# Rearranging the first loads of a SwiGLU kernel: one x load, a load issued behind the sigmoid, and a transposing load held by a dependency

## Chip, cores, metric

One core of a Trainium2 chip. The metric is the device time of one execution in microseconds (us), as a median over several executions. A lower time is better. Where two kernels are compared, "fast" executions are used: those that are not over 1.5% above the fastest of the same kernel.

## The reference

```python
B, S, D, F = 32, 32, 512, 1792        # x: (32, 32, 512), all bf16
def reference(x, w1, w3, w2):
    gate = jnp.einsum("bsd,df->bsf", x, w1)
    up = jnp.einsum("bsd,df->bsf", x, w3)
    h = _silu(gate) * up
    out = jnp.einsum("bsf,fd->bsd", h, w2)
    return out
```

There are 1024 rows of x. The kernel works on them in two blocks of 512, and on the first block's first chunk of weights in half-blocks of 256.

## The kernel before

The part that matters is the start, where nothing can be computed until bytes have arrived. `x_sb` holds the first 256 rows of x as they lie in memory; TensorE turns them with an identity matrix, and VectorE and ScalarE copy the result into `xT`. The next 256 rows come straight into `xT` through a transposing load. "w1's first half" below means the dts (128-row slices of the contraction) 0 and 1 of its first four column tiles, and "second half" the dts 2 and 3; each is 256 KB (0.26 MB). SP and ScalarE each have a queue of loads. "Gates" and "ups" below are the matmuls of x with w1 and with w3, "turns" the matmuls that turn x; a load "lands" when its data has arrived, and `fo` counts the column tiles.

```python
    load_x(nc.sync, 0, 1)                                   # 128 KB
    load_x(nc.scalar, 1, 2)                                 # 128 KB
    load_w(nc.sync, w1_sb, w1_v, 0, FK, 0, 2)               # w1 first half, 256 KB
    nc.scalar.activation(table[:], one, SIGMOID)            # brings the sigmoid's table in early
    load_w(nc.scalar, w1_sb, w1_v, 0, FK, 2, DT)            # w1 second half
    load_w(nc.sync, w3_sb, w3_v, 0, FK, 0, 2)               # w3 first half
    load_w(nc.sync, w3_sb, w3_v, 0, FK, 2, DT)              # w3 second half
    nc.sync.dma_start_transpose(out=xT[:, :, HB:NB], in_=x_flat[HB:NB, :])
    # ... the rest of w1 and w3, the second transposing load, w2: all on SP
    # ... warm-up matmuls, the turns of x and their four copies
    gates = [bank("gate_ps", "gate") for _ in range(FK)]
    for dt in range(DT):
        for fo in range(FK):
            project(gates[fo], w1_sb, fo, 0, HB, [dt])      # 16 gate matmuls, first half-block
    ups = [bank("up_ps") for _ in range(FK)]
    for dt in range(DT):
        for fo in range(FK):
            project(ups[fo], w3_sb, fo, 0, HB, [dt])        # 16 up matmuls, first half-block
    for fo in range(FK):                                    # second half-block: needs the transposing load
        project(gates[fo], w1_sb, fo, HB, NB, range(DT), HB)
        project(ups[fo], w3_sb, fo, HB, NB, range(DT), HB)
        swiglu(gates[fo], ups[fo], fo, 0)
    # ... everything after this is one unbroken row of matmuls
```

Of the kernel before, what the change touches and what calls it, by code (L numbers as in the profile page):

```python
# [10 lines left out]
def kernel(  # L11
# [8 lines left out]
    nc = tc.nc  # L20
    P = nc.NUM_PARTITIONS
    fp32 = mybir.dt.float32
    bf16 = mybir.dt.bfloat16
    SIGMOID = mybir.ActivationFunctionType.Sigmoid
# [3 lines left out]
    N = B * S  # L28
    NB = 512
    HB = NB // 2  # L30
    DT = D // P
    FT = F // P
# [4 lines left out]
    x_flat = x.flatten_outer_dims()  # L37
    out_flat = out.flatten_outer_dims()
    w1_v = w1.rearrange("(dt p) f -> p dt f", p=P)
    w3_v = w3.rearrange("(dt p) f -> p dt f", p=P)  # L40
    w2_v = w2.rearrange("(ft p) d -> p ft d", p=P)

    consts = ctx.enter_context(tc.tile_pool(name="consts", bufs=1))
# [5 lines left out]
    x_view = x_flat.rearrange("(nt p) d -> p nt d", p=P)  # L49
    ident = consts.tile([P, P], bf16, name="ident")  # L50
    make_identity(nc, ident[:])
    x_sb = consts.tile([P, HB // P, D], bf16, name="x_sb")
    xT = consts.tile([P, DT, N], bf16, name="xT")
    w1_sb = consts.tile([P, DT, F], bf16, name="w1_sb")
    w3_sb = consts.tile([P, DT, F], bf16, name="w3_sb")
    w2_sb = consts.tile([P, FT, D], bf16, name="w2_sb")
    hT = consts.tile([P, FT, N], bf16, name="hT")

    FK = 4

    def load_x(queue, t0, t1):
        queue.dma_start(out=x_sb[:, t0:t1, :], in_=x_view[:, t0:t1, :])  # L62

    def load_w(queue, w_sb, w_v, c0, c1, d0=0, d1=DT):
        f0, f1 = c0 * P, c1 * P
        queue.dma_start(out=w_sb[:, d0:d1, f0:f1], in_=w_v[:, d0:d1, f0:f1])

    one = nc.const_aps.tensor(1.0, [P, 1], bf16)
    table = consts.tile([P, 1], fp32, name="table")

    load_x(nc.sync, 0, 1)
    load_x(nc.scalar, 1, 2)
    load_w(nc.sync, w1_sb, w1_v, 0, FK, 0, 2)
    nc.scalar.activation(table[:], one, SIGMOID)  # L74
    load_w(nc.scalar, w1_sb, w1_v, 0, FK, 2, DT)
    load_w(nc.sync, w3_sb, w3_v, 0, FK, 0, 2)
    load_w(nc.sync, w3_sb, w3_v, 0, FK, 2, DT)
    nc.sync.dma_start_transpose(out=xT[:, :, HB:NB], in_=x_flat[HB:NB, :])
    for c0, c1 in ((FK, 8), (8, FT)):
        load_w(nc.sync, w1_sb, w1_v, c0, c1)  # L80
        load_w(nc.sync, w3_sb, w3_v, c0, c1)
    nc.sync.dma_start_transpose(out=xT[:, :, NB:N], in_=x_flat[NB:N, :])
    FH = FT // 2
    nc.sync.dma_start(out=w2_sb[:, 0:FH, :], in_=w2_v[:, 0:FH, :])
    nc.sync.dma_start(out=w2_sb[:, FH:FT, :], in_=w2_v[:, FH:FT, :])

    def bank(name, tag="any"):
        return psum.tile([P, NB], fp32, name=name, tag=tag)
# [26 lines left out]
    def put(copy, pT, dts, nts):  # L115
        copy(  # L116
            xT[:, dts[0] : dts[-1] + 1, nts[0] * P : (nts[-1] + 1) * P],
            pT[:].rearrange("p d t c -> p d (t c)"),
        )
# [21 lines left out]
    parts = [turned(dts, nts) for _, dts, nts in plan]  # L141
    for pT, (copy, dts, nts) in zip(parts, plan):
        put(copy, pT, dts, nts)
    gates = [bank("gate_ps", "gate") for _ in range(FK)]
    for dt in range(DT):
        for fo in range(FK):
# [18 lines left out]
    for nt in range(NT):  # L165
        last = nt == NT - 1
        c0 = 0
        for DB in (D // 2, D // 4, D // 4) if last else (D,):
# [12 lines left out]
            else:  # L181
                nc.scalar.copy(o_sb[:], o_ps[:])  # L182
            nc.sync.dma_start(
                out=out_flat[nt * P : (nt + 1) * P, c0 : c0 + DB],
                in_=o_sb[:],
# [32 lines left out]
```

## Time and profile before

| what | before |
|---|---|
| median of 3 runs, then of 6 | 82.28, 82.16 us |
| span of the profiled execution | 80.6 us (that execution took 82.39) |
| TensorE busy | 94% of the span |
| gates of the first half-block start | 5.07 us |
| ups start | 6.83 us |
| second half-block starts | 8.57 us |

How to read it: from 5.07 us on TensorE has no wait worth naming, so the kernel's time is the moment at which the matmuls can start, plus a fixed rest. The start of the second half-block (8.57 us) is a good single number for that moment. The prediction below shows the lines of the page, the chain and the windows on which this rests.

### The profile page before, as it was taken

The page shows a single profiled execution, that of the slowest core. Times are in us where ns is not written, and L with a number is a line of the kernel's source. Part 1 is how long each engine was busy: PE and PEld are TensorE (multiplying, and loading weights), DVE is VectorE, ACT ScalarE, POOL GpSimd, SP SyncE. Part 2 cuts the span into 40 slices and gives each one's busy share as a digit, 9 for nine tenths or more (in the row PEclk, how much of TensorE's full clock was granted, in tenths as well). Part 3 has the DMA queues.
Part 4 walks back from the last instruction along what each step waited for, and adds up shares of the span by engine and source line. Part 5 has one row for each costly group of instructions (what it writes and reads, how often), then busy time and mean ns, then how long its engine had stood idle before and what let it go on. Part 6 is the DMA issues. An engine that isn't in the chain of part 4 may idle for free.

```text
span 80.6 us, 1063 instructions
## 1 busy us (share of the span) xinstructions
PE 75.9 (94%) x404; PEld 38.8 (48%) x410; DVE 39.4 (49%) x61; ACT 23.2 (29%) x39; POOL 0.7 (1%) x6
## 2 busy tenths in 40 slices
PE   6959999999999999999999999999999999999960
PEld 2348984444444444444444444444444444444850
DVE  0110189999888878878868878872000000000040
ACT  4430274223432223432223432220220220220200
POOL 3000000000000000000000000000000000000000
PEclk9999999999999999999999999999999999999999
DMA  1999999989910000000000000000101102001120
GB/s 24 271 365 273 350 370 370 295 185 355 355 47 0 0 0 0 0 0 0 8 4 0 0 0 0 0 4 0 38 27 65 41 24 73 34 31 65 36 78 17
DMA packets 9893, 7.67 MB, mean 95 GB/s; under 512 B 3744, under 2 KB 9888, under 8 KB 9888
## 3 DMA queue, kind: packets, MB, share of 16 engines
q1 hardware_dynamic: 9472, 7.21, 29.6%
q10 hardware_dynamic: 416, 0.39, 1.4%
q8 instruction: 3, 0.05, 0.3%
q14 instruction: 2, 0.02, 0.1%
HBM read 5.77 MB, written 1.05 MB: 85 GB/s over the span
## 4 chain that ended last, share of the span: by engine, by line
PE 90%; DMA 5%; issue 1%; SPq 0%; DVE 0%; DVEq 0%
PE gate_ps L123 30%; PE o_ps L171 30%; PE up_ps L123 30%; DMA w_sb<-in_w_dram 5%; SPq L62 0%; DVE o_sb L180 0%; DVEq L180 0%
## 5 line engine op out<-in xcount | busy, mean ns | idle before, releaser
L123 PEld LDWEIGHTS <-w_sb 128*128 128x128 bf16 x256 | 25.0, 98 | 24.2 <-DMA w_sb<-in_w_dram 1.1
L123 PE MATMUL gate_ps<-xT,w_sb 128*128 128x512 bf16 (+1 forms) x126 | 28.7, 352 | 1.0 <-DMA w_sb<-in_w_dram 0.9
L123 PE MATMUL up_ps<-xT,w_sb 128*128 128x512 bf16 (+1 forms) x126 | 28.7, 352 | 0.1
L133 ACT ACTIVATE sig<-gate_ps 128x512 f32<-128x512 f32 x28 | 16.7, 597 | 32.0 <-PE gate_ps L123 29.7
L171 PE MATMUL o_ps<-w_sb,hT 128*128 128x512 bf16 (+2 forms) x138 | 24.3, 336 | 0.1
L135 DVE TENSOR_TENSOR t<-gate_ps,sig 128x512 f32<-128x512 f32 x28 | 19.3, 689 | 9.5 <-ACT sig L133 9.5
L136 DVE TENSOR_TENSOR hT<-t,up_ps 128x512 bf16<-128x512 f32 x28 | 19.3, 688 | 3.3 <-PE gate_ps L123 0.5
L171 PEld LDWEIGHTS <-hT 128*128 128x128 bf16 x140 | 12.6, 98 | 12.0
L180 DVE CAST o_sb<-o_ps 128x128 bf16<-128x128 f32 (+1 forms) x3 | 1.0, 336 | 22.3 <-PE o_ps L171 22.3
L182 ACT CAST o_sb<-o_ps 128x512 bf16<-128x512 f32 x7 | 4.1, 586 | 17.9 <-PE o_ps L171 17.9
L94 PE MATMUL warm_ps<-const-bfloat16-1.0 128*128 128x512 bf16 x6 | 2.7, 626 | 0.8 <-PEq L202 0.8
L116 DVE CAST xT<-pT 128x128 bf16<-128x128 f32 (+1 forms) x2 | 0.7, 358 | 3.7 <-PE pT L106 3.7
L94 PEld LDWEIGHTS <-const-bfloat16-1.0 128*128 128x128 bf16 x6 | 0.7, 136 | 1.8 <-issue 1.8
L74 ACT ACT_TABLE_LOAD x1 | 1.3, 1283 | 1.2 <-PEq L202 1.2
L116 ACT CAST xT<-pT 128x128 bf16<-128x128 f32 (+1 forms) x2 | 0.9, 426 | 1.2 <-PE pT L106 1.2
L106 PEld LDWEIGHTS <-x_sb 128*128 128x128 bf16 x8 | 0.5, 101 | 0.9 <-DMA x_sb<-in_x_dram 0.8
L106 PE MATMUL pT<-ident,x_sb 128*128 128x128 bf16 x8 | 0.7, 230 | 0.0
masks.py:199 POOL TENSOR_SCALAR_AFFINE_SELECT ident<-ident 128x128 bf16<-128x128 bf16 x1 | 0.3, 294 | 0.1
masks.py:197 POOL MEMSET ident<- 128x128 bf16 x1 | 0.2, 205 | 0.3 <-POOLq L202 0.3
L74 ACT ACTIVATE table<-const-bfloat16-1.0 128x1 f32<-128x1 bf16 x1 | 0.2, 203 | 0.0
L202 POOL MEMSET const-bfloat16-1.0<- 128x1 bf16 x1 | 0.1, 103 | 0.0
L202 POOL MEMSET const-uint8-127<- 128x1 uint8 x1 | 0.1, 103 | 0.0
(2 smaller groups left out, 0.2 us busy)
## 6 DMA issues: line engine op xcount, KB each, us to landing
w_sb<-in_w_dram SPq DMA_DIRECT2D x2, 896.0 KB, 7.0
w_sb<-in_w_dram SPq DMA_DIRECT2D x2, 768.0 KB, 8.1
w_sb<-in_w_dram SPq DMA_DIRECT2D x2, 512.0 KB, 5.8
out_dram<-o_sb SPq DMA_DIRECT2D x7, 128.0 KB, 1.7
w_sb<-in_w_dram SPq DMA_DIRECT2D x3, 256.0 KB, 4.3
w_sb<-in_w_dram ACTq DMA_DIRECT2D x1, 256.0 KB, 4.0
x_sb<-in_x_dram ACTq DMA_DIRECT2D x1, 128.0 KB, 2.8
x_sb<-in_x_dram SPq DMA_DIRECT2D x1, 128.0 KB, 2.6
```

The source lines that it names most:

```text
L74: nc.scalar.activation(table[:], one, SIGMOID)
L94: nc.tensor.matmul(warm_ps[:, 0:cols], lhsT=one.to_broadcast([P, P]), rhs=one.to_broadcast([P, cols]), start=True, stop=True,)
L106: nc.tensor.matmul(pT[:, i, j, :], lhsT=x_sb[:, nt, dt * P : (dt + 1) * P], rhs=ident[:], start=True, stop=True,)
L116: copy(xT[:, dts[0] : dts[-1] + 1, nts[0] * P : (nts[-1] + 1) * P], pT[:].rearrange("p d t c -> p d (t c)"),)
L123: nc.tensor.matmul(ps[:, c0 : c0 + n1 - n0], lhsT=w_sb[:, dt, fo * P : (fo + 1) * P], rhs=xT[:, dt, n0:n1], start=(dt == 0), stop=(dt == D ...
L133: nc.scalar.activation(sig[:], gate_ps[:], SIGMOID)
L135: nc.vector.tensor_mul(t[:], gate_ps[:], sig[:])
L136: nc.vector.tensor_mul(hT[:, fo, nb * NB : (nb + 1) * NB], t[:], up_ps[:])
L171: nc.tensor.matmul(o_ps[:], lhsT=hT[:, fo, nt * P : (nt + 1) * P], rhs=w2_sb[:, fo, c0 : c0 + DB], start=(fo == 0), stop=(fo == FT - 1),)
L180: nc.vector.tensor_copy(o_sb[:], o_ps[:])
L182: nc.scalar.copy(o_sb[:], o_ps[:])
L202: nc = _bacc.Bacc("TRN2", target_bir_lowering=False, num_devices=1)
```

## The change

Its intent is to have only two loads on each queue at first, so that x and w1's first half come undisturbed: x goes in one load on SP, w1's first half follows it there. ScalarE's two loads (w1's second half, all of w3) wait until the sigmoid has run, because the sigmoid now writes into the place where w1's second half will land. The transposing load would now stand in another queue than w3, so it is held back: it must wait for a one-column GpSimd copy into its destination, which reads the first copied column of `xT`.

```diff
-    table = consts.tile([P, 1], fp32, name="table")
-
-    load_x(nc.sync, 0, 1)
-    load_x(nc.scalar, 1, 2)
+
+    nc.sync.dma_start(out=x_sb[:], in_=x_view[:, 0 : HB // P, :])
     load_w(nc.sync, w1_sb, w1_v, 0, FK, 0, 2)
-    nc.scalar.activation(table[:], one, SIGMOID)
+    nc.scalar.activation(w1_sb[:, 2, 0:1], one, SIGMOID)
     load_w(nc.scalar, w1_sb, w1_v, 0, FK, 2, DT)
-    load_w(nc.sync, w3_sb, w3_v, 0, FK, 0, 2)
-    load_w(nc.sync, w3_sb, w3_v, 0, FK, 2, DT)
-    nc.sync.dma_start_transpose(out=xT[:, :, HB:NB], in_=x_flat[HB:NB, :])
-    ... (the later loads on SP, moved down unchanged)
+    load_w(nc.scalar, w3_sb, w3_v, 0, FK)
 ... (after the turns and copies of x)
+    nc.gpsimd.tensor_copy(xT[:, 0, HB : HB + 1], xT[:, 0, 0:1])
+    nc.sync.dma_start_transpose(out=xT[:, :, HB:NB], in_=x_flat[HB:NB, :])
+    ... (the later loads on SP)
```

More of the change, by code (lines that the diff above doesn't have):

```diff
@@ L59 @@
     FK = 4
-    def load_x(queue, t0, t1):
-        queue.dma_start(out=x_sb[:, t0:t1, :], in_=x_view[:, t0:t1, :])
     def load_w(queue, w_sb, w_v, c0, c1, d0=0, d1=DT):
@@ L68 @@
     one = nc.const_aps.tensor(1.0, [P, 1], bf16)
-    table = consts.tile([P, 1], fp32, name="table")
-    load_x(nc.sync, 0, 1)
-    load_x(nc.scalar, 1, 2)
+    nc.sync.dma_start(out=x_sb[:], in_=x_view[:, 0 : HB // P, :])
     load_w(nc.sync, w1_sb, w1_v, 0, FK, 0, 2)
-    nc.scalar.activation(table[:], one, SIGMOID)
+    nc.scalar.activation(w1_sb[:, 2, 0:1], one, SIGMOID)
     load_w(nc.scalar, w1_sb, w1_v, 0, FK, 2, DT)
-    load_w(nc.sync, w3_sb, w3_v, 0, FK, 0, 2)
-    load_w(nc.sync, w3_sb, w3_v, 0, FK, 2, DT)
-    nc.sync.dma_start_transpose(out=xT[:, :, HB:NB], in_=x_flat[HB:NB, :])
-    for c0, c1 in ((FK, 8), (8, FT)):
-        load_w(nc.sync, w1_sb, w1_v, c0, c1)
-        load_w(nc.sync, w3_sb, w3_v, c0, c1)
-    nc.sync.dma_start_transpose(out=xT[:, :, NB:N], in_=x_flat[NB:N, :])
-    FH = FT // 2
-    nc.sync.dma_start(out=w2_sb[:, 0:FH, :], in_=w2_v[:, 0:FH, :])
-    nc.sync.dma_start(out=w2_sb[:, FH:FT, :], in_=w2_v[:, FH:FT, :])
+    load_w(nc.scalar, w3_sb, w3_v, 0, FK)
     def bank(name, tag="any"):
@@ L143 @@
         put(copy, pT, dts, nts)
+    nc.gpsimd.tensor_copy(xT[:, 0, HB : HB + 1], xT[:, 0, 0:1])
+    nc.sync.dma_start_transpose(out=xT[:, :, HB:NB], in_=x_flat[HB:NB, :])
+    for c0, c1 in ((FK, 8), (8, FT)):
+        load_w(nc.sync, w1_sb, w1_v, c0, c1)
+        load_w(nc.sync, w3_sb, w3_v, c0, c1)
+    nc.sync.dma_start_transpose(out=xT[:, :, NB:N], in_=x_flat[NB:N, :])
+    FH = FT // 2
+    nc.sync.dma_start(out=w2_sb[:, 0:FH, :], in_=w2_v[:, 0:FH, :])
+    nc.sync.dma_start(out=w2_sb[:, FH:FT, :], in_=w2_v[:, FH:FT, :])
     gates = [bank("gate_ps", "gate") for _ in range(FK)]
```

## The prediction

> **What bounds the kernel now.** I read the page first, for the bound and the chain that ended last. TensorE is busy for 94% of the span, and 90% of the chain is its matmuls:
>
> ```profile
> PE 75.9 (94%) x404; PEld 38.8 (48%) x410; DVE 39.4 (49%) x61; ACT 23.2 (29%) x39; POOL 0.7 (1%) x6
> PE 90%; DMA 5%; issue 1%; SPq 0%; DVE 0%; DVEq 0%
> ```
>
> The chain over the first 15 us says which transfer starts it (start, length, what):
>
> ```profile
> 0.74 0.39 SPq L62
> ...
> 1.20 3.83 DMA w_sb<-in_w_dram
> 5.02 0.05 issue
> 5.07 1.92 PE gate_ps L123 x16
> 6.99 1.75 PE up_ps L123 x16
> 8.74 0.44 PE gate_ps L123 x4
> ```
>
> From 5.07 us TensorE never stops again: the view of waits has one wait of a projection on a DMA in the whole run.
>
> ```profile
> PE gate_ps L123 <- DMA w_sb<-in_w_dram: 0.9, 1, 0.9
> ```
>
> So only the first nine microseconds can change. The work after them is serial: anything gained or lost at the start of the second half-block (8.57 us in the timeline) goes into the time one for one. For each load, I put its issue (start, length) beside its landing (the last number of a line is us from issue to landing), in narrow windows. The second half of w3 and the transposing load:
>
> ```profile
> 2.16 0.47 SPq L66 DMA_DIRECT2D w_sb<-in_w_dram  x1
> w_sb<-in_w_dram SPq DMA_DIRECT2D x1, 256.0 KB, 4.6
> 2.67 1.30 SPq L78 DMA_TRANSPOSE xT<-in_x_dram  x1
> xT<-in_x_dram SPq DMA_TRANSPOSE x1, 5.1
> ```
>
> By the same reading: x lands at 3.3 and 3.5, w1's halves at 1.20 + 3.8 = 5.0 (SP) and 1.23 + 4.0 = 5.2 (ScalarE), w3's first half at 1.66 + 4.3 = 6.0, its second at 2.16 + 4.6 = 6.76, the transposing load at 2.67 + 5.1 = 7.77. The up matmuls start at 6.83 and need w3's second half only after eight matmuls (0.11 us each, since 16 take 1.75), at 7.7; so today it has 0.9 us to spare. The last view is the DMA rate by windows (last column GB/s, before it the DMA share):
>
> ```profile
> 3.00:3.25 0.25, 0.25 (x2) 0.00 (x0) 0.00 (x0) 0.00 (x0) 0.00 (x0) 1.00 0.69 189
> 4.00:4.50 0.50, 0.14 (x3) 0.00 (x0) 0.38 (x2) 0.43 (x2) 0.00 (x0) 1.00 1.07 373
> 5.50:6.00 0.50, 0.50 (x7) 0.44 (x6) 0.00 (x0) 0.00 (x0) 0.00 (x0) 1.00 1.05 349
> 6.00:6.50 0.50, 0.50 (x7) 0.44 (x5) 0.00 (x0) 0.00 (x0) 0.00 (x0) 1.00 1.38 238
> ```
>
> The bytes run at 350 to 380 GB/s from 3.25 us, whichever queue issued them. Summing rate times width over all such windows gives 1.32 MB at 6.0 us, which is x + w1 + w3 for this block (0.26 + 0.52 + 0.52 MB = 1.31 MB). So the start is a saturated stream in order of need, and the dip to 238 GB/s after 6.0 is the transposing load: 392 packets between 6.2 and 6.7 us, 389 of them under 512 B, about 20 ns per packet on each of 16 engines.
>
> **What the Trainium skill says.** "DMA: Bandwidth & Descriptors", Issuing engines are not separate DMA queues: loads from several engines run on the same 16 DMA engines, and a second issuer saves only issue time. The trace agrees: both queues together move 375 GB/s between 3.6 and 4.6 us, and SP's alone moves 356 GB/s between 4.9 and 5.3. The same page, Queues, rings and completion order: each DMA engine goes round-robin between its queues by packets and takes one queue in order. In the kernel before, the transposing load is in the same queue as w3, behind it, so no trace here shows what happens when it is in another. "ScalarE: Activation LUTs", What ACT_TABLE_LOAD costs, has about 1283 ns for the load plus some 1380 ns of drain; the trace has 1283 ns, and the activation follows at 2.46 us directly on the load's end (1.17 + 1.28 = 2.45), with no drain to be seen. I use the trace. "TensorE: Matmul & The Clock Gate", Part 1, has a full clock after some 3.4 us of activity and a half one after some 3.4 us of idling. The warm-up matmuls fit it (0.43 us per 512 columns, later 0.22); the gap that I expect below is far shorter than that.
>
> **The change part by part.**
> 1. x in one load on SP instead of two. The same 0.26 MB; an issue of 0.45 us (like the 256 KB issues) instead of 0.40. It lands at about 3.4 to 3.5 us, and the first turn cannot start on the early half (3.34 now): +0.1 us on the turns and copies, which end at 4.76 now. A gate can start when dt 0 is copied, at about 4.4.
> 2. The half of w1 on ScalarE waits for the sigmoid, as that now writes into its place. Without the x load in front, the table load starts at about 0.75 instead of 1.17, and the activation ends at 0.75 + 1.28 + 0.20 = 2.23, so the load goes out at about 2.3 instead of 1.23. From issue to first byte takes some 1.1 us (x issued 0.74, bytes from about 1.9), so its bytes start at 3.5. SP's half no longer shares: x's bytes end at about 3.0, 0.1 us of dip, then 0.26 MB at 360 GB/s = 0.73 us, to 3.8, landing by about 4.4 instead of 5.03. ScalarE's half follows directly and lands at about 5.2 to 5.3, as before.
> 3. So gates start at about 4.45 instead of 5.07 (0.6 us earlier); the second half of their dts is needed at 4.45 + 0.88 = 5.33, just in time. Gates end at about 6.2.
> 4. w3 is one load behind that half. The first up matmul now needs all of it, not its first half. Its last byte cannot come earlier than now, as the same 1.31 MB must come first: 6.76 at best. This eats the gain: TensorE waits from 6.2 to at least 6.8, and ups begin where they begin today.
> 5. The transposing load waits for one VectorE copy (ends at 4.01 now, 4.1 after) and a one-column GpSimd copy (0.10 us, as its 128x1 memset, plus a signal on each side): issue at about 4.4, bytes from about 5.5, by the same 1.1 us. At that point some 0.17 MB of w3 are still to come (349 GB/s over 0.5 us), and now from the other queue, so the two take turns. 170 packets of 1 KB are 11 per DMA engine; with one small packet between each two that is 11 x 20 ns = 0.22 us more; with turns of equal bytes it is up to 0.17 MB / 240 GB/s = 0.7 us. I take 0.2 to 0.3, with up to 0.1 for a bubble ahead of ScalarE's half and signals.
> 6. Transposed x lands no later than now by bytes (all 1.57 MB lie ahead of it either way), about 7.8 to 8.3; it is needed when ups end, 7.1 + 1.75 = 8.85. The later loads are issued up to 1.6 us later on SP, but their bytes stand in line anyway: w1's next chunk lands at 4.02 + 5.3 = 9.3 and is needed at 12.07, w3's at 4.64 + 6.2 = 10.8 and needed at 12.93. 2 us of slack; nothing there.
>
> Sum: ups start at 6.76 + about 0.3 = 7.05 to 7.1 instead of 6.83: 0.25 us lost. 82.28 + 0.25 = 82.5 us.
>
> **The rivals.** (a) No collision, and w3 lands early: the transposing load is slower to its first byte than a plain one (its issue takes 1.30 us, not 0.45), so w3 is through before it. Then ups begin between 6.2 (no wait at all) and 6.8: 0.6 to 0 us gained, 81.7 to 82.3. For it: the long issue. Against the full 0.6: the DMA engines were already full, so nothing can bring the bytes sooner. (b) Turns of equal bytes or worse: w3 lands at about 7.4, 0.6 us lost, 82.9. For it: a DMA share of 1.38 in the transposing window says that it holds the engines long for few bytes. (c) The transposing load, issued 1.7 us later, becomes the wait: from 4.4, with today's 5.1 us, it would land at 9.5, against a need at 8.85; 0.9 us lost in all, 83.2. Against it: most of the 5.1 us was standing behind w3 (its bytes start only at about 5.5 to 6.0). (d) ScalarE's half of w1 is late because the table load doesn't start earlier: gates pause some 0.4 us in their middle; the wait for w3 hides it, unless w3 is pushed too, by the same bubble.
>
> **Range and chances.** Even (a) at its best is 0.7% faster, so 2% (1.65 us) is out of reach on that side. On the other side (b) and (c) together make about 1.3 us. Three runs of before spread over 0.57 us, which puts some 0.3 us on a median. I take 81.8 to 83.2, with 1% for faster, 95% for within 2%, 4% for slower.
>
> **What would show it right or wrong.** The chain should start with x or SP's half of w1, gates at 4.4 to 4.6, then a new wait of the up matmuls on a DMA into w3 of 0.6 to 1.2 us, ups starting at 6.8 to 7.4; the second half-block 1.75 us later without a wait. The ScalarE load of w1 should be issued at 2.2 to 2.4 and w3's at about 2.8; packets under 512 B should appear together with w3's in the other queue between 5.5 and 6.3 us. I am wrong in size if w3 lands before 6.7, wrong in mechanism if the gates wait for xT or w1 beyond 4.7, or if a wait on the transposing load appears at the second half-block, or if anything after 12 us waits for a load.

## The result, and the profile after

The changed kernel takes 83.37 us (83.13 to 83.99, 6 runs), against 82.16 (82.04 to 82.61, 6 runs) for the kernel before. The ratio is 1.0147, with an interval of 1.0106 to 1.0188. Ratios here are formed from the fast runs of the same rounds, so they are not quite the ratio of the medians quoted beside them. It is a clear loss of about 1.2 us, and the time lies above the predicted range (81.8 to 83.2).

The chain of the changed kernel over its first 10 us (start, length, what):

```profile
0.73 1.28 ACT L69
...
2.03 0.21 ACT w_sb L69
...
2.26 0.41 ACTq L63
...
2.71 4.89 DMA w_sb<-in_w_dram
7.64 1.92 PE up_ps L109 x16
9.56 0.44 PE gate_ps L109 x4
```

It no longer starts with SP's half of w1. It starts with ScalarE's table load and sigmoid, passes through the issue of w1's second half, and then stands for 4.89 us on the load of w3, issued at 2.71 and landed at 7.59. Ups start at 7.64 instead of 6.83. From there on it is as before: the timeline has the second half-block at 9.39 instead of 8.57, with no wait in between.

The first loads of the changed kernel, one line for each issue (last number: us from issue to landing). They were issued at 0.74, 1.25, 2.26 and 2.71 us:

```profile
x_sb<-in_x_dram SPq DMA_DIRECT2D x1, 256.0 KB, 2.8
w_sb<-in_w_dram SPq DMA_DIRECT2D x1, 256.0 KB, 3.0
w_sb<-in_w_dram ACTq DMA_DIRECT2D x1, 256.0 KB, 3.7
w_sb<-in_w_dram ACTq DMA_DIRECT2D x1, 512.0 KB, 4.9
```

x landed at 3.55 and w1's first half at 4.2, as intended (5.03 before), and gates started at 4.42. But w1's second half landed only at 5.96 (5.27 before), and w3, whole, at 7.59 (its second half at 6.78 before). The reason stands in the rates. First the kernel before, then the changed one, in windows of half a microsecond; the last column is GB/s, the one before it the mean busy share of the 16 DMA engines:

```profile
3.00:3.50 0.50, 0.50 (x3) 0.10 (x1) 0.00 (x0) 0.00 (x0) 0.00 (x0) 1.00 0.89 268
3.50:4.00 0.50, 0.50 (x8) 0.40 (x7) 0.28 (x2) 0.16 (x1) 0.00 (x0) 1.00 1.06 367
4.50:5.00 0.50, 0.00 (x0) 0.00 (x0) 0.00 (x0) 0.26 (x1) 0.00 (x0) 1.00 1.09 383
```

```profile
3.00:3.50 0.50, 0.49 (x2) 0.00 (x0) 0.00 (x0) 0.00 (x0) 0.00 (x0) 1.00 1.06 363
3.50:4.00 0.50, 0.41 (x5) 0.41 (x6) 0.08 (x1) 0.00 (x0) 0.00 (x0) 1.00 0.80 184
4.00:4.50 0.50, 0.50 (x7) 0.50 (x6) 0.47 (x2) 0.27 (x1) 0.19 (x1) 1.00 0.76 150
4.50:5.00 0.50, 0.50 (x5) 0.38 (x3) 0.16 (x1) 0.34 (x1) 0.00 (x0) 1.00 0.69 145
5.00:5.50 0.50, 0.50 (x5) 0.32 (x3) 0.00 (x0) 0.25 (x1) 0.00 (x0) 1.00 0.97 291
6.00:6.50 0.50, 0.50 (x6) 0.45 (x6) 0.00 (x0) 0.00 (x0) 0.00 (x0) 1.00 1.10 388
```

SP's two loads run at full rate up to about 3.5 us. Then ScalarE's queue takes over, alone, and the stream falls to 145 to 184 GB/s for a microsecond and a half before it recovers. Before, the same stretch ran at 367 to 383. From 3.5 to 5 us the changed kernel moves about 160 GB/s on average against 374: 214 GB/s over 1.5 us are 0.32 MB less, or 0.86 us of full rate. Another 0.1 us is lost from 5 to 6, and some 0.13 had been gained between 3.0 and 3.5 (363 against 268). The sum, 0.83 us, agrees with what w3's landing moved: 7.59 - 6.78 = 0.81. This is a count of bytes, not an experiment: no run below takes the loss of rate out of the changed kernel without another cost.

The trace also records each piece of a load with its duration. In the normal stream a piece of 1 KB takes 46 ns. In the slow stretch the median is still 46 ns, but 23 pieces (between 3.5 and 5.5 us) take over 100 ns, some of them 500 to 720, and the engines are idle in between. In the kernel before there are 2 such pieces in the same 2 us. I call this stretch "the slow phase". What follows is about what makes it. (Long pieces as such are nothing new: at their start, from 1.5 to 3.5 us, both kernels have about as many, 24 before and 25 after.)

One more thing differs in the trace, and is hidden by the wait for w3. The first gates of the changed kernel stand 0.21 us apart until 5.5 us and 0.11 us after that; before, they stood 0.11 us apart from the start. Twice the spacing is called "the half clock" below. The granted clock in the windows reads 1.00 all the while, so it does not show this.

The two traces show 0.8 to 0.9 us of the 1.2 (spans 80.6 and 81.5). Most of the rest is that the profiled execution of the kernel before took 82.39 us, 0.23 over its median, while that of the changed kernel, 83.36, sat at its median.

### The profile page after: what moved, and what is told of

It is laid out like the page before. It is cut to its first block, busy times and chain, and to the rows that moved or that the text cites. A ratio compares the mean times of both kernels' runs of the same rounds, so it can differ in the third digit from the quotient of the medians.

```text
span 81.5 us, 1062 instructions
## 1 busy us (share of the span) xinstructions
PE 77.0 (94%) x404; PEld 39.2 (48%) x410; DVE 39.4 (48%) x61; ACT 23.2 (28%) x39; POOL 0.9 (1%) x7
## 2 busy tenths in 40 slices
DMA packets 9862, 7.67 MB, mean 94 GB/s; under 512 B 3713, under 2 KB 9857, under 8 KB 9857
## 4 chain that ended last, share of the span: by engine, by line
PE 87%; DMA 6%; ACT 2%; issue 1%; ACTq 1%; DVE 0%; DVEq 0%
PE up_ps L109 30%; PE o_ps L168 30%; PE gate_ps L109 27%; DMA w_sb<-in_w_dram 6%; ACT L69 2%; ACTq L63 1%; DVE o_sb L177 0%; ACT w_sb L69 0%; DVEq L177 0%
## 5 line engine op out<-in xcount | busy, mean ns | idle before, releaser
L109 PE MATMUL gate_ps<-xT,w_sb 128*128 128x512 bf16 (+1 forms) x126 | 29.4, 358 | 0.1
```

Source lines behind the costliest of these rows:

```text
L109: nc.tensor.matmul(ps[:, c0 : c0 + n1 - n0], lhsT=w_sb[:, dt, fo * P : (fo + 1) * P], rhs=xT[:, dt, n0:n1], start=(dt == 0), stop=(dt == D ...
```

## The experiments

Eighteen kernels ran, in five calls on four chips; each call has runs of the kernel before beside it (medians 82.44, 82.70, 82.56, 82.38, 82.44; the third call's are the second's and one more). Ratios to the kernel before compare better than times. All results were correct. "Last landed" below is the moment at which the last of the 16 DMA engines had reported.

### Undoing one part of the changed kernel

**e1_no_hold**: ScalarE issues at once, the sigmoid runs afterwards.

```diff
-    nc.scalar.activation(w1_sb[:, 2, 0:1], one, SIGMOID)
     load_w(nc.scalar, w1_sb, w1_v, 0, FK, 2, DT)
     load_w(nc.scalar, w3_sb, w3_v, 0, FK)
+    nc.scalar.activation(table[:], one, SIGMOID)
```

> The changed kernel, but ScalarE issues its half of w1 and w3 at once and does the sigmoid afterwards into a tile of its own. Theory R (a queue that starts from empty runs at some 150 GB/s for its first microsecond or more; the hold puts ScalarE's slow start behind SP's, where it is alone): both slow starts now fall together before 2.5 us, the rate stays at 340 GB/s or more from 2.5 to 6 us, w3 lands at 6.5 to 6.9 instead of 7.59, ups start at 6.6 to 7.0 (7.64 in the changed kernel), time 82.2 to 82.6. Rival T (the transposing load in the other queue makes w3 late): it still stands in the other queue behind a small copy, so ups start at 7.4 or later and the time stays above 83.0.

Measured: 84.01 us in the median, but in two groups, 83.14 to 83.23 and 84.78 to 85.44; ratio of the fast runs 1.0087 (1.0041 to 1.0132). The trace is of a slow run, so I use it only for the bytes. The slow phase at 3.5 us is indeed gone (369 to 385 GB/s from 3.5 to 5.5), but the start is slower than in the changed kernel (160 and 272 GB/s in the half microseconds from 2.5 and 3.0), and ScalarE's loads now take turns with SP's: x lands at 4.81 and w1's first half at 6.00. So the hold does what it is meant to do, protect x and w1's first half, and removing it moves the loss rather than cures it. In this slow run's trace the gates also ran at the half clock, up to 8.8 us; whether that is what parts the two groups is not shown, as no trace of a fast run was kept. The expected time was missed.

**e2_w3_halves**: w3 in two loads.

```diff
-    load_w(nc.scalar, w3_sb, w3_v, 0, FK)
+    load_w(nc.scalar, w3_sb, w3_v, 0, FK, 0, 2)
+    load_w(nc.scalar, w3_sb, w3_v, 0, FK, 2, DT)
```

> The changed kernel, but w3 comes in two loads on ScalarE, as before it did on SP. Both theories leave the byte stream as it is (slow between 3.6 and 5 us). If the wait for the whole of w3 is what turns the late stream into time, ups start right behind the gates at about 6.9 and the time is 82.5 to 82.8, 0.6 to 0.8 below the changed kernel. If not (first half late as well), ups start after 7.3 and the time is above 83.0.

Measured: 82.82 us, ratio 1.0035 (0.9997 to 1.0073). By the medians this is 0.55 us below the changed kernel, by the ratios 0.9, though in other rounds, and the interval no longer excludes the time of the kernel before. The slow phase is there as before the edit (164 and 201 GB/s from 4.0 to 5.0), so the waiting for the whole of w3 is what turns a good part of it into time. The trace, of the slowest of the six runs, shows less, 0.15 us (ups at 7.49, not 7.64): in it w1's second half landed only at 6.56, with half of its engines done at 5.54, and the gates waited for it:

```profile
2.26 4.30 DMA w_sb<-in_w_dram
```

**e3_t_free**: the transposing load not held.

```diff
+    nc.sync.dma_start_transpose(out=xT[:, :, HB:NB], in_=x_flat[HB:NB, :])   # on SP, right behind w1's first half
     nc.scalar.activation(w1_sb[:, 2, 0:1], one, SIGMOID)
 ...
-    nc.gpsimd.tensor_copy(xT[:, 0, HB : HB + 1], xT[:, 0, 0:1])
```

> The changed kernel without the hold on the transposing load: it stands on SP right behind its half of w1. Theory R: its bytes come from about 3.6 us beside ScalarE's slow start and take what that leaves free, so the sum of the rates rises between 3.6 and 5 us, small packets stand there, and w3 ends no more than 0.4 us later than in the changed kernel (7.6 to 8.0), time 83.2 to 83.8. Rival T (small packets are what costs): w3 ends some 1 us later still, at 8.5, time 84.2 or more.

Measured: 89.22 us (87.87 to 89.83), ratio 1.073 (1.0643 to 1.0816). The two fast runs have 87.87 and 89.09; the trace is of a slow one (89.23), with the same loss. Both theories were far too mild. The chain has the load of w3:

```profile
2.77 8.93 DMA w_sb<-in_w_dram
```

and the windows of this kernel while the transposing load and ScalarE's loads are in flight together:

```profile
4.50:5.00 0.50, 0.06 (x1) 0.00 (x0) 0.09 (x1) 0.41 (x1) 0.00 (x0) 1.00 0.57 69
5.00:5.50 0.50, 0.00 (x0) 0.00 (x0) 0.00 (x0) 0.18 (x1) 0.00 (x0) 1.00 1.15 94
```

The stream falls to 69 to 158 GB/s between 4 and 6.5 us. The 1024 pieces of the transposing load take from 3.58 to 7.98 us; alone (e11 below) they take from 9.32 to 10.94. Both loads suffer. w3 landed at 11.70, 4.1 us later than in the changed kernel. The 16 ups after it ran at the half clock and took 3.60 us instead of 1.92, so that about 1.7 of the 5.9 us between the two spans are the clock's. The small GpSimd copy is no decoration: with w3 in the other queue, it is what keeps the changed kernel (83.37) from losing another 4.5 to 5.7 us.

**e9_swap**: the two halves of w1 change queues, to see whether the slow phase belongs to those rows.

```diff
-    load_w(nc.sync, w1_sb, w1_v, 0, FK, 0, 2)
+    load_w(nc.sync, w1_sb, w1_v, 0, FK, 2, DT)
-    nc.scalar.activation(w1_sb[:, 2, 0:1], one, SIGMOID)
-    load_w(nc.scalar, w1_sb, w1_v, 0, FK, 2, DT)
+    nc.scalar.activation(w1_sb[:, 0, 0:1], one, SIGMOID)
+    load_w(nc.scalar, w1_sb, w1_v, 0, FK, 0, 2)
 ... (the first gates take the dts in the order 2, 3, 0, 1)
```

> The changed kernel with the halves of w1 swapped: SP brings dts 2 and 3, ScalarE (held) 0 and 1, and the first gates take the dts in the order 2, 3, 0, 1. Theory W (the rows of w1's second half are slow to read the first time, whichever queue): the slow phase moves to 3.0 to 4.3 us on SP and ScalarE's load then runs at 340 GB/s or more. Theory P (it is the place in the stream, after half a megabyte, or the queue): SP runs at 340 GB/s or more to 3.5 us and the slow phase stays at 3.6 to 5 us as in the changed kernel; time 83.0 to 83.6 again.

Measured: 83.47 us, ratio 1.0091 (1.003 to 1.0152), ups at 7.76. SP ran at 377 and 389 GB/s from 2.5 to 3.5, ScalarE's load at 113 and 145 from 4.0 to 5.0. The slow phase stays in its place; theory W falls.

**e13_touch**: the rows of w1's second half are read once, 32 B each, ahead of the sigmoid.

```diff
+    primer = consts.tile([P, 2, 16], bf16, name="primer")
+    nc.scalar.dma_start(out=primer[:], in_=w1_v[:, 2:DT, 0:16])
     nc.scalar.activation(w1_sb[:, 2, 0:1], one, SIGMOID)
```

> The changed kernel with a tiny load (8 KB, 32 B out of each row of w1's second half, into a tile that nobody reads) on ScalarE's queue ahead of the sigmoid. If the slow phase is the first reading of those rows, or the first use of ScalarE's queue, it is gone: 320 GB/s or more from 3.5 to 5 us, w3 lands at 6.7 to 7.0, ups start at 6.8 to 7.1, time 82.4 to 82.8. If it is the place in the stream, nothing moves: ups at 7.5 to 7.8, time 83.2 to 83.6.

Measured: 83.36 us, ratio 1.0078 (1.0026 to 1.013), ups at 7.78. There was a full stretch at 340 GB/s from 4.5 to 5.0, but 70 before it and 236 to 274 after it, when w3 began. Neither first use of the queue nor first reading of these rows alone explains it.

**e22_touch_pool**: the same idea for w1's second half and w3, from GpSimd's queue.

```diff
+    nc.gpsimd.dma_start(out=primer[:, 0:2, :], in_=w1_v[:, 2:DT, 0:16])
+    nc.gpsimd.dma_start(out=primer[:, 2:6, :], in_=w3_v[:, :, 0:16])
```

> The changed kernel, with two tiny loads issued by GpSimd behind the making of the identity, which read 32 B out of each row of w1's second half and of w3 into a tile that nobody uses, so that those rows have been read once when ScalarE's loads start. Theory F: the slow phase from 3.6 to 5 us shrinks to the 0.3 us or so in which ScalarE's queue starts; w3 lands at 6.7 to 7.1 instead of 7.59, ups start at 6.8 to 7.2, time 82.5 to 82.9. Theory P: ups at 7.5 or later as in the changed kernel, 83.2 to 83.7, or worse by what the 768 tiny pieces cost.

Measured: 83.78 us, ratio 1.0175 (1.0138 to 1.0213). Ups started at 8.30, later than without it; from 3.5 to 6 us the stream ran at 213 to 276 GB/s. As a remedy it failed. As a test it is weak: only 32 pieces of GpSimd's queue that are large enough to count show in the trace, the first at 3.52 us, so it is not shown that the rows were read ahead of their turn.

### Putting the loads into one queue, or two

**e4_one_queue**: all four first loads on SP.

```diff
-    nc.scalar.activation(w1_sb[:, 2, 0:1], one, SIGMOID)
-    load_w(nc.scalar, w1_sb, w1_v, 0, FK, 2, DT)
-    load_w(nc.scalar, w3_sb, w3_v, 0, FK)
+    load_w(nc.sync, w1_sb, w1_v, 0, FK, 2, DT)
+    load_w(nc.sync, w3_sb, w3_v, 0, FK)
+    nc.scalar.activation(table[:], one, SIGMOID)
```

> The changed kernel, but all four first loads stand on SP in order of need (x, both halves of w1, w3 whole), the sigmoid into a tile of its own; the transposing load still held by the small copy. Theory R: only one slow start, before 2.5 us; 340 GB/s or more from 2.5 to 6 us, w1's second half lands at about 5.0, w3 at 6.3 to 6.7, ups start at 6.4 to 6.8, time 81.8 to 82.3, as fast as before or faster. Rival (one queue alone cannot fill the engines, two are needed): the rate falls below 250 GB/s after 3.5 us and the time is above 83.

Measured: 83.67 us, ratio 1.0138 (1.0099 to 1.0177). This was the surprise that overturned my first theory (theory R, a queue that starts from empty): SP's queue never ran empty here, all four loads had been issued by 2.72 us, and still the stream fell to 260 and 182 GB/s from 4.0 to 5.0, after the first half megabyte:

```profile
DMA packets 91, 0.09 MB, mean 182 GB/s; under 512 B 2, under 2 KB 91, under 8 KB 91
```

The rival, that one queue alone cannot fill the engines, had the right numbers but does not hold either: the same queue ran at 373 GB/s from 2.5 and at 359 from 5.5. The phase is milder than at a handover (in the changed kernel 150 and 145), so the start of ScalarE's queue may add to it.

**e10_w3_first**: one queue, another order.

```diff
+    load_w(nc.sync, w3_sb, w3_v, 0, FK, 0, 2)
+    load_w(nc.sync, w1_sb, w1_v, 0, FK, 2, DT)
+    load_w(nc.sync, w3_sb, w3_v, 0, FK, 2, DT)
```

> As the one-queue kernel, but in the order x, w1 first half, w3 first half, w1 second half, w3 second half, all on SP. There the slow phase came with w1's second half, from 3.77 us. Theory W (it belongs to those rows): 3.5 to 4.3 us at 340 GB/s or more while w3 is read, slow after that. Theory P (place in the stream): slow from 3.75 to 5 us while w3's first half is read. Either way gates wait until 5.5 to 6.5 for w1's second half; time 82.8 to 84.

Measured: 83.68 us, ratio 1.0109 (1.0047 to 1.0172). 264, 211 and 236 GB/s from 3.5 to 5.0, while w3's first half was read. With e9 this settles that the slow phase follows the place in the stream, not the rows. Whether the place is "the third load" or "after half a megabyte" these two cannot tell, as both come to the same here.

**e11_t_after_w3**: e4 with the transposing load released only by w3's landing.

```diff
-    nc.gpsimd.tensor_copy(xT[:, 0, HB : HB + 1], xT[:, 0, 0:1])
+    nc.gpsimd.tensor_copy(xT[:, 0, HB : HB + 1], w3_sb[:, 0, 0:1])
```

> As the one-queue kernel, but the small copy that releases the transposing load reads w3, so it is issued only when w3 has landed. In the one-queue kernel w3's first engine was done at 6.17 us and half of them only at 7.70, with transposing packets beside. If the transposing load holds up w3's end, w3 now lands at 6.5 to 6.9 (7.79 there) and ups start at 6.6 to 7.0; the transposing load is then issued at about 6.9 and lands 3 to 4 us later, so the second half-block waits for it until 10 to 11 and the time is 83.5 to 85. If w3 is late by its own bytes, it lands at 7.5 or later again.

Measured: 85.51 us, ratio 1.0346; the second half-block waited 1.8 us for the transposing load, as foreseen. Landing of w3 in the two kernels, from the records of the 16 engines:

```
                    first engine   8th     last
e4_one_queue            6.17       7.70    7.79
e11_t_after_w3          6.16       6.92    7.67
```

The transposing load does hold up half of the engines (7.70 against 6.92), but the last engine would be late without it. In e11 the stream trickles at 123 and then 29 GB/s from 6.5 to 7.5: a few engines are still at work on their share of w3 while the others have finished. A load has landed only when its slowest engine has, and the slow phase leaves the engines unequal.

**e14_two_busy**: both queues busy at once, w1 on SP, w3 on ScalarE.

```diff
-    nc.scalar.activation(w1_sb[:, 2, 0:1], one, SIGMOID)
-    load_w(nc.scalar, w1_sb, w1_v, 0, FK, 2, DT)
-    load_w(nc.scalar, w3_sb, w3_v, 0, FK)
+    load_w(nc.sync, w1_sb, w1_v, 0, FK, 2, DT)
+    load_w(nc.scalar, w3_sb, w3_v, 0, FK, 0, 2)
+    load_w(nc.scalar, w3_sb, w3_v, 0, FK, 2, DT)
+    nc.scalar.activation(table[:], one, SIGMOID)
```

> The changed kernel with both queues busy from the start, but not with the halves of w1 side by side: x and both halves of w1 on SP, both halves of w3 on ScalarE at once (the sigmoid follows into a tile of its own), the transposing load held by the small copy. Theory A2 (two queues with work hide the slow phase): the sum of the rates stays at 340 GB/s or more from 3.5 to 5.5 us. Rival (only reading w1's halves side by side avoids it): a microsecond under 250 GB/s between 3.5 and 5.5 us. w1's second half lands at about 6 either way, time 82.5 to 84.

Measured: 84.47 us, ratio 1.0195 (1.0127 to 1.0264); the trace is of a slow run and again used for the bytes alone. 354 to 389 GB/s from 3.5 to 6.0, so no slow phase there; but 158 and 307 in the half microseconds from 2.5 and 3.0, where a lone SP queue runs at 360. Two queues that started together paid at the start instead.

### Bursts in a quiet stretch

**e6_quiet**: the kernel before, with bursts into an unused tile in the second block, when the DMA engines have nothing else to do.

```diff
+    def quiet(queue, s):                       # 256, 256 and 512 KB on one queue
+        queue.dma_start(out=scr[:, s : s + 2, :], in_=w1_v[:, 0:2, 0:NB])
+        queue.dma_start(out=scr[:, s + 2 : s + 4, :], in_=w1_v[:, 2:DT, 0:NB])
+        queue.dma_start(out=scr[:, s + 4 : s + 8, :], in_=w3_v[:, :, 0:NB])
 ... (after the swiglu of fo 1: ScalarE's queue; of fo 5: SP's; of fo 9: 512 KB on ScalarE and twice 256 KB on SP)
```

> The kernel before, with three bursts of loads into a tile that nobody reads, in the second block, when the DMA engines are otherwise idle: 1 MB on ScalarE's queue alone in pieces of 256, 256 and 512 KB, the same on SP's queue alone, and 512 KB on each at once. Theory A2 (a queue working alone has a slow phase, first packets of 300 to 700 ns, after its first half megabyte or at its start; two queues hide it): each of the single bursts shows a window of 0.5 us or more under 250 GB/s after its first 0.5 us, the double burst none. Rival (the slow phase belongs to the first microseconds of the execution): after a start of less than 0.75 us all three run at 340 GB/s or more to their end.

Measured (one look, 82.19 us). The windows of the burst on ScalarE's queue alone, then of the double burst:

```profile
33.00:33.50 0.50, 0.50 (x4) 0.25 (x3) 0.40 (x2) 0.00 (x0) 0.00 (x0) 1.00 0.47 86
34.00:34.50 0.50, 0.50 (x4) 0.23 (x3) 0.28 (x1) 0.18 (x1) 0.00 (x0) 1.00 1.07 375
35.00:35.50 0.50, 0.50 (x4) 0.20 (x2) 0.49 (x1) 0.19 (x1) 0.00 (x0) 1.00 0.79 137
36.00:36.50 0.50, 0.50 (x4) 0.26 (x3) 0.50 (x1) 0.00 (x0) 0.00 (x0) 1.00 0.96 336
...
47.00:47.50 0.50, 0.50 (x4) 0.27 (x3) 0.40 (x1) 0.10 (x1) 0.00 (x0) 1.00 0.81 55
48.00:48.50 0.50, 0.50 (x5) 0.20 (x3) 0.47 (x1) 0.00 (x0) 0.00 (x0) 1.00 1.06 377
49.00:49.50 0.50, 0.50 (x4) 0.22 (x3) 0.50 (x1) 0.38 (x1) 0.00 (x0) 1.00 1.09 385
```

The slow phase is reproduced 33 us into the run, with nothing else going on: slow start, full rate for the first half megabyte, then 137 GB/s. SP's queue alone does the same. The double burst has a longer slow start (up to about 47.75 us) and then runs at 377 to 385 to its end. So the rival, that it belongs to the first microseconds of an execution, falls.

**e19_quiet_sizes**: bursts of 2 MB on SP's queue, in four loads of 512 KB, in pieces of 1 KB and then of 2 KB.

```diff
+    for i in range(4):   # 512 pieces of 1 KB each
+        nc.sync.dma_start(out=scr[:, 4 * i : 4 * i + 4, :], in_=w1_v[:, :, i * 384 : i * 384 + NB])
 ... (later: four loads of 256 pieces of 2 KB from w3)
```

> The kernel before with two bursts of 2 MB on SP's queue alone in the quiet second block: first four loads of 512 KB in pieces of 1 KB (512 pieces each), then four of 512 KB in pieces of 2 KB (256 each). In the earlier quiet bursts of 1 KB pieces the slow phase came after the first half megabyte, 512 pieces or 32 for each DMA engine, 2 us after the first byte. If it goes by pieces, the second burst has it after 1 MB, some 3 us after its first byte. If it goes by bytes or by time, the second burst has it after 0.5 MB, or 2 us after its first byte, as the first has. If it comes back after every half megabyte, the first burst shows it three times, if only once after a queue has been empty, once.

Measured (one look, 82.27 us); the first burst, with the half megabyte reached at 36.0 us:

```profile
34.50:35.00 0.50, 0.50 (x4) 0.20 (x2) 0.50 (x1) 0.00 (x0) 0.00 (x0) 1.00 0.83 205
35.50:36.00 0.50, 0.50 (x4) 0.26 (x3) 0.35 (x1) 0.50 (x1) 0.00 (x0) 1.00 1.08 381
36.50:37.00 0.50, 0.50 (x5) 0.21 (x3) 0.40 (x2) 0.00 (x0) 0.00 (x0) 1.00 1.09 389
```

There is no slow phase at all after the start, in either burst (2 KB pieces: 406 to 414 GB/s from 45.5 to 47.0). That was in neither column of my expectation. Its start, though, is longer, about 1.2 us from the first byte to full rate, against 0.7 us in the bursts that begin with 256 KB loads. So the slow phase does not go by bytes, by pieces or by time alone.

**e20_quiet_touch**: four loads of 256 KB on SP's queue, three times, with and without rows that had just been read.

```diff
+    if nb == 1 and fo == 1:
+        burst(0, (w1_v, w1_v, w1_v, w1_v))     # dts 0-1, 2-3, and the same again
+    if nb == 1 and fo == 5:
+        burst(8, (w1_v, w1_v, w3_v, w3_v))
+    if nb == 1 and fo == 9:
+        burst(16, (w3_v, w3_v, w1_v, w1_v))
```

> The kernel before with three bursts of four loads of 256 KB on SP's queue alone in the quiet second block, all of the same shape: the first reads w1's rows 0 to 255, 256 to 511, and the same two again (into other places); the second the same two of w1 and then the two of w3; the third w3's two and then w1's two. Theory F (what is slow is the first reading of rows that have not been read lately; each engine's first pieces of the first two loads are waited for together at the start, those of the third load at its start): after the start the first burst runs at 340 GB/s or more to its end, the second and third have half a microsecond or more under 250 GB/s after half a megabyte. Theory P (it is the third load after a queue has been empty, whatever it reads): all three have it.

Measured (one look, 82.55 us); the first burst, which reads the same rows twice:

```profile
35.00:35.50 0.50, 0.50 (x4) 0.21 (x3) 0.40 (x2) 0.03 (x1) 0.00 (x0) 1.00 1.07 365
35.50:36.00 0.50, 0.50 (x4) 0.26 (x3) 0.35 (x1) 0.50 (x1) 0.00 (x0) 1.00 0.85 201
36.00:36.50 0.50, 0.50 (x4) 0.21 (x3) 0.40 (x1) 0.07 (x1) 0.00 (x0) 1.00 0.82 199
```

All three bursts have it, at half a megabyte (the others fall to 217 and 234). Theory F, first reading of rows, falls; what is slow is what follows the first two 256 KB loads on one queue, whatever it reads.

### Parts of the change on the kernel before

**e5_before_hold**: only the hold of w1's second half.

```diff
-    nc.scalar.activation(table[:], one, SIGMOID)
+    nc.scalar.activation(w1_sb[:, 2, 0:1], one, SIGMOID)
```

> The kernel before with one part of the change: ScalarE's half of w1 held behind the sigmoid (which writes into it), all else as before, w3 on SP. Theory A (any load that goes alone on its queue starts with long packets of 300 to 700 ns and holds the stream at 150 to 250 GB/s for about a microsecond; another queue with work fills the engines meanwhile): SP's w3 fills them, so the sum of the rates stays above 300 GB/s from 3.5 to 5 us, gates wait for w1's second half until 5.5 to 6, ups follow at once, and the time is 82.1 to 82.7. Rival (the hold itself, by where it puts w1's second half in time, slows the whole stream): the sum falls below 250 GB/s for a microsecond and the time is 83 or more.

Measured: 85.05 us in the median of four, of which two are fast (84.31 and 84.33), against 82.70 in the same rounds. My theory A expected 82.1 to 82.7, so it falls, and the rival is borne out: the stream fell to 203, 172 and 234 GB/s from 3.5 to 5.0 while SP read w3. Then w1's second half came together with the transposing pieces, which nothing held here, and landed at 7.84:

```profile
2.70 5.15 DMA w_sb<-in_w_dram
```

**e15_x_one**: only the single x load.

```diff
-    load_x(nc.sync, 0, 1)
-    load_x(nc.scalar, 1, 2)
+    load_x(nc.sync, 0, 2)
```

> The kernel before with one part of the change: x's first half in one load on SP, so that ScalarE's queue begins with its half of w1. If the single x load is harmless, 82.2 to 82.7 and w1's first half at 5.0 to 5.3. If ScalarE's half of w1 now comes ahead of x in time and takes half of its bandwidth (as in the kernel without the hold, where x landed at 4.8), the turns start near 4, the gates near 5.5, and the time is 82.8 to 83.6.

Measured: 84.09 us, ratio 1.0177 (1.0125 to 1.0228). ScalarE's queue now begins with w1's second half beside x, and x lands at 4.19 instead of 3.52. From 3.5 to 6 us the stream runs at 367 to 383: no slow phase. But the chain shows a second cost:

```profile
5.37 3.16 PE gate_ps L122 x16
8.53 1.75 PE up_ps L122 x16
```

Gates start only 0.3 us later than before, but take 3.16 us instead of 1.92: their matmuls stand 0.21 us apart instead of 0.11, the spacing of the half clock. The spacing fell to 0.11 us only at 8.0 us. The turns had waited for x, to 4.24 us, but whether TensorE's idling is the reason is not shown: in e16 the turns started at 3.37, as early as before, and the spacing fell at 6.4.

**e16_w3_whole**: only w3 in one load.

```diff
-    load_w(nc.sync, w3_sb, w3_v, 0, FK, 0, 2)
-    load_w(nc.sync, w3_sb, w3_v, 0, FK, 2, DT)
+    load_w(nc.sync, w3_sb, w3_v, 0, FK)
```

> The kernel before with one part of the change: w3's first part in one load instead of two, on SP as before. By the stream of before it lands at 6.76, as its second half does there; gates end at 6.83 there, so ups wait 0 to 0.1 us: 82.2 to 82.7, no difference. If the transposing load behind it in the same queue holds up its last engines (as in the one-queue kernel, 7.79), ups start at 7.2 or later and the time is 82.7 to 83.5.

Measured: 83.11 us, ratio 1.0089 (1.0054 to 1.0123). w3 landed at 7.16 rather than 6.78, which would cost 0.3 to 0.4 us; the stream had dipped to 264 GB/s from 4.5 to 5.0. In this trace it is hidden by the half clock: gates ran from 4.83 to 7.52 (2.69 us). So I cannot say how much of the 0.7 us is w3's; that one load is no gain here is shown.

**e17_t_held**: only the hold of the transposing load and what follows it on SP.

```diff
+    nc.gpsimd.tensor_copy(xT[:, 0, HB : HB + 1], xT[:, 0, 0:1])
     nc.sync.dma_start_transpose(out=xT[:, :, HB:NB], in_=x_flat[HB:NB, :])   # with all later loads, moved behind the copies of x
```

> The kernel before with one part of the change: the transposing load and all that follows it on SP held by the small GpSimd copy. It is issued at about 4.4 instead of 2.67, its bytes start at about 6.2 (1.8 us later, as in the changed kernel), when w3 is through; it lands at about 7.9 and is needed at 8.57: 82.2 to 82.7. If it comes later than needed, a wait on it appears at the second half-block and the time is 83 or more.

Measured: 82.40 us, ratio 0.9988 (0.9951 to 1.0025). It is harmless, as expected: the transposing load was issued at 4.34, landed at 7.57 and was needed at 8.55.

**e12_by_dt**: an attempt to beat the kernel before, w1 in four loads in the order of need.

```diff
-    load_w(nc.sync, w1_sb, w1_v, 0, FK, 0, 2)
+    load_w(nc.sync, w1_sb, w1_v, 0, FK, 0, 1)
+    load_w(nc.sync, w1_sb, w1_v, 0, FK, 2, 3)
+    load_w(nc.scalar, w1_sb, w1_v, 0, FK, 1, 2)
+    load_w(nc.scalar, w1_sb, w1_v, 0, FK, 3, DT)
     nc.scalar.activation(table[:], one, SIGMOID)
-    load_w(nc.scalar, w1_sb, w1_v, 0, FK, 2, DT)
```

> An attempt to beat the kernel before: as before, but w1's first part in four loads, one for each dt, 0 and 2 on SP, 1 and 3 on ScalarE, so that both queues bring it in the order in which the gates need it. dts 0 and 1 should land at 4.2 to 4.5 instead of 5.03, gates start at 4.4 to 4.6 instead of 5.07, all else is hidden behind them: 81.6 to 82.0, some 0.4 below before. It is no better than before if every load lands as late as the last of its queue's neighbours.

Measured: 82.71 us, ratio 0.9993 (0.9947 to 1.0039). The bytes came as planned (dt 0 at 4.00 us), and the gates started 0.7 us earlier than before (4.35 in the timeline; the chain counts from the end of the turns). It shows where that went:

```profile
4.56 2.76 PE gate_ps L125 x16
7.32 1.75 PE up_ps L125 x16
```

The 16 gates took 2.76 us, at the half clock until 6.5. In this trace, starting the matmuls earlier was worth nothing, as they ran at half speed. I found no version that beats the kernel before, beyond e17, which equals it.

## Why the prediction was wrong

It had the direction and the place of the new wait, but not the cause of the loss, and the size was three to five times too small: 0.25 us foreseen, 0.8 in the traces, 1.2 in the medians. The 0.25 us stood for the transposing load and w3 taking turns; what was lost is the full rate at the handover from SP's queue to ScalarE's. By its own test ("wrong in mechanism if the gates wait for xT or w1 beyond 4.7") the mechanism was wrong, as the gates waited for w1 at 6.0 us. That the new wait, 0.58 us, is close to the lower end of the 0.6 to 1.2 forecast is luck: it began and ended 0.7 to 0.8 us later than foreseen.

- **Part 1 and the first half of part 2 held.** x landed at 3.55 (said 3.4 to 3.5), ScalarE's load was issued at 2.26 (said 2.3), w1's first half landed at 4.2 (said 4.4), gates started at 4.42 (said 4.45).
- **The step that failed is the rest of part 2**: "ScalarE's half follows directly and lands at about 5.2 to 5.3, as before", and with it part 4's claim that w3 comes at "6.76 at best" and ups "begin where they begin today", and part 5's "up to 0.1 for a bubble ahead of ScalarE's half". The half landed at 5.96, and the bubble was the slow phase: about 0.8 us net by the byte count above, where the prediction allowed 0.1. I had seen that the stream before was saturated from 3.25 us "whichever queue issued them", and took this as a property of the DMA engines. It held only for that arrangement of loads. The dips in the kernel before, at 2.0 to 2.5 us and at 3.0, were in the view I read; I noted one as "0.1 us of dip" and did not ask what would make it longer.
- **Part 3 held in its start and failed in its end.** The prediction took gates 0.11 us apart from the first and set the clock aside ("the gap that I expect below is far shorter"). The first six stood 0.21 us apart, and gates ended at about 6.9, not 6.2. The wait for w3 hid it; the half clock also hid part of the late w1, which was needed at 5.86 instead of 5.33.
- **Part 4's mechanism held.** One load of w3 makes ups wait for all of it: splitting it (e2) gives back 0.55 us by the medians, 0.9 by the ratios, 0.15 in the one trace.
- **Part 5 had the wrong moment.** The transposing load was issued at 4.49 (said 4.4), but its first piece came at 6.32, not 5.5: from issue to first piece it took 1.83 us, not 1.1 as a plain load, and 1.30 of that was the issue itself. Rival (a) had named the longer issue as its ground. So it met only w3's tail. That turns are taken one 1 KB piece against one small piece, on which the estimate of 0.22 us rests, no run shows. How much it cost there is not shown separately; the 0.8 us are accounted for without it. What a full collision costs is shown by e3: w3 4.1 us later, far more than the 0.6 of rival (b).
- **Part 6 held.** It landed at 8.6 and was needed at 9.39; no later load was waited for. Rival (c) did not happen.
- **Rival (d)** was the right thought with the wrong cause. The gates did pause (0.26 us of a wait for weights at 6.0 us), though the table load had started at 0.73, as foreseen. The wait for w3 hid it.
- **What stays open** is the cause of the slow phase. Shown in single traces: it is not the rows (e9, e10), not ScalarE's queue (e4, e6), not an empty queue (e4), not the first microseconds of an execution (e6), not rows read for the first time (e20), not bytes or pieces alone (e19). It came wherever a stream began with 256 KB loads on one queue, with the third load. In the kernel before, e15 and e17, where both queues had loads of w1 at the same time, it did not come. But two queues are not enough: e5 had it, e12, with 128 KB loads on both, had 232 and 293 GB/s from 4 to 5 us, and e16 264 from 4.5. A stream that began with loads of 512 KB had a longer start and no slow phase. That each stream pays about a microsecond, at once or in two parts, would fit most of these, but it is only argued. What the quiet bursts suggest, w1's first part in one load of 512 KB in the changed kernel itself, was not tried.

## What to carry to other kernels

The full rate of the DMA stream belonged here to an arrangement of loads, not to the DMA engines alone: read the rate in half-microsecond windows, and before you reorder the first megabyte, measure the new order in a quiet stretch of the same kernel. A transposing load in flight beside plain loads of another queue put w3 back by 4.1 us here (e3), so a cheap dependency that keeps it back is worth having wherever the two could meet. A load lands when its slowest engine does (in e11 the first was done at 6.16 and the last at 7.67), so try to split a load that a whole stage waits for.

## What the Trainium skill lacked or had wrong

- **"DMA: Bandwidth & Descriptors"**: it describes no slow phase within a stream. With one queue at work at a time, a stream that began with 256 KB loads ran, after its start, at about 370 GB/s to the half megabyte and then at 137 to 266 for a microsecond or more, in the changed kernel (184, 150, 145) and in quiet bursts (137 and 266 in e6, 201 and 199 in e20); a stream of 512 KB loads did not (342 to 389 GB/s from 35 to 40 us, e19).
- The same page says in its rules that a transpose next to ordinary DMAs needs nothing. It says so of the data being right, and for that it agrees with all runs. Of the time it says nothing there, and something is needed: with plain loads in the other queue the transposing pieces took 4.4 us instead of 1.6, the stream fell to 69 GB/s, and w3 landed 4.1 us later (e3).
- The same page has a first byte at about 0.6 us on these queues and does not say from when. Here the first piece of the first plain load came 1.1 us after the start of its issue (0.74 to 1.83) and 0.64 after the end of it, so the figure fits if it counts from the end. For the transposing load the first piece came 1.83 us after the start of its issue in the changed kernel and 1.38 in e11.
- **"TensorE: Matmul & The Clock Gate"**: the clock's rise is said to vary by the phase of a window of some 3.4 us. Here, by the spacing of the matmuls, it came 2.8 us after the first warm-up matmul at the earliest (e5), 5.7 us in e12, though TensorE had stood idle for no more than 0.2 us of them, 7.3 in e15, and 14.6 at the latest (e3, a slow run, with long waits).
- **"ScalarE: Activation LUTs"**: it counts a drain of some 1380 ns with every switch of tables. In both kernels, where the table is loaded for the first time and not switched, nothing of it is to be seen: the sigmoid started 0.01 us after the load's end.
